# A conditioned attention and mixer block: the product of w_v and G as plain 32-bit matmuls, and every operation in a new place

## The chip, the core and the metric

The kernel runs on one core of a Trainium2 chip. The core has a matmul engine (PE in the profile, whose weight loads are shown apart as PEld), a vector engine (DVE), an engine for activation functions and scaled copies (ACT), a general engine (POOL), and an engine that here only issues DMA transfers (SP). Each takes its own instructions in the order in which the program gives them, and waits at an instruction until what it needs has been done elsewhere. Operands lie in on-chip memory, and matmul results in the accumulator banks (PSUM). The metric is the device time of one execution in microseconds (us).

## The reference

The input is x with 2048 rows (tokens) of 512 columns, a conditioning vector c, and the weights of two blocks. Cut to what matters:

```python
mod = (silu(c) @ w_mod).reshape(1, 6, 1, -1)           # sa, ca, ga, sb, cb, gb
h = layernorm(x) * (1 + ca) + sa
q, k, v = h @ wqkv, split into 32 heads of 16 columns
pq, pk = phi(q), phi(k)                                # phi(t) = t + 1 where t > 0, else exp(t); + 1e-6
kv = einsum("bhsd,bhse->bhde", pk, v);  z = pk summed over the tokens
o = (pq @ kv) / (pq . z + 1e-6)                        # head by head
x = x + ga * (o @ wo)
h = layernorm(x) * (1 + cb) + sb
z = gelu(h @ w_in);  z1 = z[:, :688];  z2 = layernorm(z[:, 688:])
g = w_sp @ z2 + b_sp                                   # w_sp is 2048 x 2048, over the tokens
out = x + gb * ((z1 * g) @ w_out)
```

## The kernel before, in words

The 2048 tokens are 16 row tiles of 128. A product that must keep the precision of 32-bit numbers is made of three: each operand is split into a high part, which is the number in the narrower 32-bit format that PE takes at its fast rate (`F32R`), and a low part, the rest; PE accumulates high times high, high times low and low times high (`mm3`, L113 to L115). A split costs a copy on ACT (L130) and a subtraction on DVE (L131), or variants of the two. A few products use plain 32-bit operands (`F32`) instead and have one matmul in the program: the modulation column `pcol` (L197), and the column means of the weights, `wm` (L335).

The stages, in the order of the program:

1. Start. w_mod gives the scale 1 + ca as a column; w_k and w_q are scaled, freed of their means and split (`mean_mm` L335, then DVE L339, then ACT L343). The first matmuls wait for the first transfers.
2. First block, per row tile: the k and q projections (`kp`, `qp`), phi, and, instead of v, G = the sum over all tokens of h (transposed) times pk, a 512 x 512 matrix that stays in accumulators (`g`).
3. After the last tile, kv = w_v (transposed) times G. Only the blocks of one head are wanted, so it is computed for four groups of 128 columns (`kv_mm`, L724 to L734: four 128-row parts `dc` of the inner dimension, four groups `g`) and masked (`kv_mask`). w_v is scaled by 1 + ca and split beforehand (`v_hi` L514, `v_lo` L518); G is split in `gh` (L702). Then kv is multiplied with w_o into m.
4. Attention output, per tile: o times m into `po`, the residual, the second layer norm, transposes, z = gelu(h2 times w_in) in two halves: z1 (L667) and z2 (`zz`, L673), layer norm of z2, and both parked in DRAM (`zd`, `z1d`). The z1 halves of the last four tiles come later (`z_late`, L872).
5. The spatial product w_sp times z2, partly plain (`Pq`) and mostly by a scheme of seven products for eight (`prod`, L956) whose operands are sums of quarters (L927 to L946); then u = z1 times the result, transposed through DRAM.
6. u times w_out (`pout`), the residual, and the output.

Nothing reorders the work. A table of two-letter names with numbers, `ORDER` for stages 1 to 4 and `ORDER3` for 5 and 6, is read from left to right; each name runs one small function, whose instructions go to the end of their engines' rows. On SP, where all transfers are issued, a transfer behind one that waits for a buffer waits with it. A second table, `SLOTS`, says which buffer of a pool each new tile takes, and so whose last use it has to wait for. The names that the prediction speaks of: `lw` loads a part of w_k or w_q and `ly` a transposed tile of x, `mr` is the column mean of a weight, `k`, `q` and `ki`, `km` belong to the projections and their weights, `kv` is the product above, `mS` and `mB` split and broadcast a modulation vector (`yh`, `yl`, then `pmod` on PE and `mod` on ACT), `g1` and `g2` are the two gelus, `d1`, `d2` and `at`, `ht` the denominator and transposes.

Of the kernel before, what the change touches and what calls it, by code (L numbers as in the profile page):

```python
# [14 lines left out]
P = 128  # L15
# [11 lines left out]
def block_kernel(ctx: ExitStack, tc: tile.TileContext, x, x_t, w_qkv, w_o, w_in, w_sp, b_sp, w_out,  # L27
# [3 lines left out]
    def pool(name, bufs, space=None, stack=None):  # L31
        if space is None:
# [21 lines left out]
        "md": "0321302313123113212312131223112131213121",  # L54
        "ta": "05431205413424204325214140532535530214014342402145025153545241503",
        "s4": (
            "076541237401267541720364615230745163074530516351065306174305264164034217563421602745032640137563"
            "017423156230764123756103625417502163256701423574635017624137135726417513064231570364712603742056"
            "34706145702614352634521670341065723410"
        ),  # L60
        "psb": "10101010101010101010110101010101010",
        "zs": "0fe123d4cba9876523d483ca9473b2dca74b2dc724d9b7c9dbc9dbc9dbc90fe165d83a4270b9c6158ef",
        "tb": (
            "065412360541631520641326542362361232134614206320606346536132613136256106313012161350420435610253"
            "256442405454132144140101063004414252053461"
        ),
        "pst": "01011010101110101",
        "st": (
            "032102312302102310232020312031320120310123102310230231131010231023102031301202130123031231012031"
            "0210"  # L70
        ),
        "ws": "0101",
        "pso": "010101001001110101011010110100101010010101010101",
        "tq": "ncedba987654mjihlkgf01327nm8gjbfcd69k0n83ebhfi4lajgmc9",
# [25 lines left out]
    def f(ap):  # L100
        return ap.bitcast(F32)
# [412 lines left out]
    def v_hi(kc):  # L514
        if not WV:
            WV.append(sb("ws", [P, 2, KC, D], F32R, "wv"))
        nc.scalar.activation(WV[0][:, 0, kc], RAW["qkv", 2, kc // 2][:, kc % 2, :], AF.Copy, scale=COL[1][:, kc:kc + 1])

    def v_lo(kc):
        nc.vector.scalar_tensor_tensor(WV[0][:, 1, kc], RAW["qkv", 2, kc // 2][:, kc % 2, :], COL[1][:, kc:kc + 1],  # L520
                                       f(WV[0][:, 0, kc]), op0=OP.mult, op1=OP.subtract)
# [19 lines left out]
    def win_lo(h, kc, eng=nc.gpsimd):  # L541
# [21 lines left out]
        "vh": v_hi, "vl": v_lo, "lW": load_win,  # L563
# [160 lines left out]
    def kv_mm(dc):  # L724
        if dc == 0:
            KV["kv"] = ps("o", [P, KC, P], "pkv")
        p, last = KV["kv"], dc == KC - 1
        for g in range(KC):
            sl = slice(g * P, (g + 1) * P)
            mm(p[:, g], WV[0][:, 0, dc, sl], GH[dc][:, 0, sl], start=dc == 0 and g == 0, stop=False,  # L730
               skip_group_check=True)
            mm(p[:, g], WV[0][:, 0, dc, sl], GH[dc][:, 1, sl], start=False, stop=False, skip_group_check=True)
            mm(p[:, g], WV[0][:, 1, dc, sl], GH[dc][:, 0, sl], start=False, stop=last and g == KC - 1,
               skip_group_check=True)  # L734
# [48 lines left out]
    def hx_lo(t):  # L783
# [16 lines left out]
        lm1,0 lm1,1 si du1 du2 du3 du4 cm1,0 lm1,2 cm1,1 cm1,2 lm1,3 cm1,3 mc lw1,0 du5 mr1,0 mr1,1 ly1 th1  # L800
        tl1 ce1 lw1,1 mr1,2 mr1,3 ly0 th0 tl0 ly2 th2 wf1,3 qh1,3 qg1,3 lw0,0 tl2 lw0,1 wf1,1 mr0,0 mr0,1
        qh1,1 qg1,1 mr0,2 wf1,0 qh1,0 lx0 mr0,3 lm0,1 s10 yp0,1 ki1,3 ki1,1 lm0,0 yp0,0 ki0,3 ki0,1 ki0,0
        kj0,1 wf1,2 lm0,2 yp0,2 ki1,0 kj1,1 lm0,3 bh0 kj0,3 qh1,2 kj1,3 ki1,2 ly5 qd1,0 wf0,0 wf0,1 wf0,3
        ya0,1 kj1,0 yp0,3 ya0,2 ya0,3 ki0,2 qh0,1 qd1,2 th5 kj1,2 qh0,0 qg0,0 kj0,0 lx1 kj0,2 lx2 s12 bh2 cr0
        ce0 qd0,1 qh0,3 s11 lx5 wf0,2 qh0,2 qg0,2 by0 kr1 bp1 by1 km2 kr2 qd0,3 qm0 tl5 km5 by2 kr0 bh1 lw2,0
        by3 bp0 ba1 ly3 s15 bx1 qr0 bb1 bp2 ba2 bl0 be1 k15 th3 bp3 qm1 qr1 ba3 bx0 lM2 tl3 km3 qm3 lx4 ka2
        ka0 s14 lx3 s13 bl1 k20 vh1 ly9 k40 ka1 lo0 th9 tl9 kr3 ly4 kh0 kl0 th4 mV2,0 mV2,1 k22 li bb0 be0 qm2
        k21 q12 bh3 gm0 tl4 ly8 k41 ks0 kh1 km4 qm4 bl2 q13 qm5 k42 ks1 ka3 k14 q22 q42 kl1 gm1 ly6 th6 kh2
        kl2 lo1 k25 k23 th8 k45 k43 mS2 q15 tl8 q14 bl3 k24 mB2 tl6 lx6 q24 lx9 ks2 ks3 kh3 qa0 k44 ks4 s16
        s19 ks5 lx8 kh4 km8 vh0 wg3 s18 km6 k16 bh9 bh5 bl5 bh4 gm2 lw2,1 q44 ly7 th7 tl7 kl3 kl4 q25 kh5 bh6  # L810
        bl4 qm6 q16 q45 k26 k46 ks6 bl9 ly12 lx7 ly11 th11 kh6 s17 ly10 q26 k18 th12 kl6 gm3 gm4 bh7 qa1 kl5
# [8 lines left out]
        kl14 bl14 lW0,2 ks15 wh0,2 mS4 zx mS3 gm13 zs bh15 zr d12 cv kh15 lX3 bl15 d10 wl0,1 kl15 d22 vb d20  # L820
        gm14 d13 gm15 gh0 gh1 gh2 q113 mB3 kv0 at2 wl0,2 gh3 d11 kv1 kv2 lW1,0 d23 mB4 wh1,1 wl1,1 kv3 kx q213
        qm15 q115 lW0,3 wh0,3 at0 d21 lW1,2 ae0 mm0 me0 ae2 mm2 me2 qm14 q114 wl0,3 at1 ae1 mm1 me1 d14 mm3
        at3 ae3 me3 d15 wh1,2 wl1,2 d24 lX0 wo0 x10 wh1,0 wl1,0 ap4 wo3 x13 wo1 h20 w02 wh1,3 wl1,3 q215 lX1
        d25 ht0 he0 w12 lX4 d17 x12 am4 ap5 ah4 al4 h22 hp2 q214 x11 am5 ah5 lX8 q413 h23 hm2 za0 zb0 g20 z00
        g10 wo4 al5 d16 h21 d19 hp3 wo5 d110 hh2 hl2 d27 d26 ht1 he1 z12 g22 q414 zl0 x14 ap6 h24 hm3 x15 z01
        g11 ap7 z02 hh3 hl3 hp4 d210 zn0 zp0 h25 g12 z13 g23 am6 ah6 hm4 hh4 am7 q415 d115 d18 z11 hp5 al6 ah7
        hl4 l5 lX7 z14 al7 d29 lX6 lX9 g21 ap10 zl2 d28 g24 zl4 d112 z04 hm5 hh5 hl5 ap8 d215 zn2 wo7 x17 g14
        h27 hp7 am8 ah8 al8 lX12 am10 z05 g15 zl3 z15 zh2 zp2 zo2 zl1 zh0 d212 d111 ah10 ap9 hm7 hh7 hl7 g25
        z03 al10 zl5 zn3 lX10 d211 wo6 x16 zp3 ap12 ap11 g13 am9 ah9 al9 zn4 d113 h26 hp6 z17 wo8 x18 z07 wo9
# [266 lines left out]
    def out_store(t, c0=0, c1=D):  # L1096
# [100 lines left out]
```

## Time and profile before

| | us |
|---|---|
| median of 3 runs | 620.19 (620.17 to 620.83) |
| span of the profiled execution, first to last instruction | 617.3 |
| PE busy in the span | 611.1 |
| DVE busy | 473.3 |
| ACT busy | 364.3 |
| POOL busy | 217.1 |

Of the profiled execution only the span is given, and its own device time isn't. The median lies 2.9 us above the span; that stands for what lies around it. The granted clock of PE was 1.000 in the mean. DMA moved 105.7 MB. A row of a view names the line of the kernel, the engine, the operation and the tile; a matmul's bar is longer than the distance to the next one, because matmuls overlap, so the pace of a row of matmuls is read from starts, or from the length of a stretch divided by their number.

### The profile page before, as it was taken

The page shows a single profiled execution, that of the slowest core. Times are in us where ns is not written, and L with a number is a line of the kernel's source. Part 1 is how long each engine was busy: PE and PEld are TensorE (multiplying, and loading weights), DVE is VectorE, ACT ScalarE, POOL GpSimd, SP SyncE. Part 2 cuts the span into 40 slices and gives each one's busy share as a digit, 9 for nine tenths or more (in the row PEclk, how much of TensorE's full clock was granted, in tenths as well). Part 3 has the DMA queues.
Part 4 walks back from the last instruction along what each step waited for, and adds up shares of the span by engine and source line. Part 5 has one row for each costly group of instructions (what it writes and reads, how often), then busy time and mean ns, then how long its engine had stood idle before and what let it go on. Part 6 is the DMA issues. An engine that isn't in the chain of part 4 may idle for free.

```text
span 617.3 us, 9528 instructions
## 1 busy us (share of the span) xinstructions
PE 611.1 (99%) x3375; PEld 558.2 (90%) x3375; DVE 473.3 (77%) x881; ACT 364.3 (59%) x619; POOL 217.1 (35%) x180
## 2 busy tenths in 40 slices
PE   8999999999999999999999999999999999999997
PEld 6788888888899999999999999999999999998886
DVE  2989889897788878988767998867757777866462
ACT  3876768565656667666566466475656564654530
POOL 0843444637676476755240012123122121300000
PEclk9999999999999999999999999999999999999999
DMA  8453323261244778646658736366455667899941
GB/s 286 174 192 117 106 69 104 75 198 40 64 121 116 206 186 223 178 136 172 194 172 277 287 133 180 104 191 181 139 171 141 196 187 167 293 280 262 291 177 68
DMA packets 91022, 105.74 MB, mean 171 GB/s; under 512 B 57088, under 2 KB 57600, under 8 KB 90976
## 3 DMA queue, kind: packets, MB, share of 16 engines
q1 hardware_dynamic: 90976, 105.15, 56.9%
q8 instruction: 26, 0.43, 0.3%
q14 instruction: 20, 0.16, 0.1%
HBM read 66.07 MB, written 25.95 MB: 149 GB/s over the span
## 4 chain that ended last, share of the span: by engine, by line
PE 89%; DVE 4%; DMA 3%; ACT 1%; SPq 1%; issue 1%; POOL 0%; DVEq 0%; ACTq 0%
PE P L956 29%; PE z L662 12%; PE Pq L956 5%; PE pout L114 3%; PE pout L113 3%; PE pout L115 3%; PE z L872 2%; PE g L113 2%; PE g L115 2%; PE qp L114 2%; PE qp L115 2%; PE qp L113 2%; PE g L114 2%; PE kp L113 2%; PE kp L114 2%; PE po L115 2%
## 5 line engine op out<-in xcount | busy, mean ns | idle before, releaser
L956 PE MATMUL P<-z,f 128*128 128x344 f32 x672 | 110.9, 320 | 0.2 <-DVE us L980 0.2
L662 PE MATMUL z<-win,ht 128*128 128x344 f32 x672 | 107.6, 320 | 0.2 <-DVE ht L301 0.2
L662 PEld LDWEIGHTS z<-win,ht 128*128 128x128 f32 x672 | 106.2, 188 | 1.1 <-DVE ht L301 0.5
L956 PEld LDWEIGHTS P<-z,f 128*128 128x128 f32 x672 | 106.6, 188 | 0.6 <-DVE us L980 0.5
L946 POOL TENSOR_TENSOR f<-raw_wsp,f 128x512 fp32r<-128x512 f32 x28 | 42.1, 1513 | 168.5 <-ACT f L943 159.3
L257 POOL TENSOR_TENSOR mv<-ve,mhalf 128x1 f32<-128x1 f32 x48 | 36.2, 757 | 43.1 <-DVE ve L256 40.7
L946 DVE TENSOR_TENSOR f<-sa,f 128x512 fp32r<-128x512 f32 x42 | 32.7, 788 | 18.8 <-ACT f L943 18.8
L943 ACT ACTIVATE f<-sa 128x512 fp32r<-128x512 f32 x42 | 26.1, 628 | 27.5 <-DVE sa L933 9.7
L943 ACT ACTIVATE f<-raw_wsp 128x512 fp32r<-128x512 f32 x56 | 34.1, 624 | 12.6 <-PE P L956 4.7
L281 ACT COPY uca<-ucb 128x768 uint16<-128x768 uint16 x32 | 31.9, 1063 | 13.5 <-DMA ucb<-uca 13.4
L480 POOL TENSOR_TENSOR pksum<-pksum,tk 128x512 f32<-128x512 f32 x15 | 23.1, 1539 | 41.4 <-DVE tk L452 34.2
L114 PE MATMUL pout<-wout,ut 128*128 128x512 f32 (+1 forms) x85 | 32.4, 381 | 0.0
L113 PE MATMUL pout<-wout,ut 128*128 128x512 f32 (+1 forms) x85 | 32.4, 381 | 0.0
L115 PE MATMUL pout<-wout,ut 128*128 128x512 f32 (+1 forms) x85 | 32.3, 380 | 0.0
L956 PE MATMUL Pq<-z,wsp 128*128 128x344 f32 x192 | 30.8, 321 | 0.0
L956 PEld LDWEIGHTS Pq<-z,wsp 128*128 128x128 f32 x192 | 30.6, 188 | 0.0
L271 ACT COPY uca<-us 128x768 uint16<-128x768 uint16 x32 | 25.0, 828 | 7.5 <-PE P L956 5.6
L591 POOL TENSOR_TENSOR prod<-pq,zrep 128x512 f32<-128x512 f32 x16 | 21.3, 1348 | 13.0 <-DMA z1d<-z 4.6
L113 PE MATMUL po<-m,pt 128*128 128x512 f32 x64 | 25.3, 396 | 0.0
L113 PE MATMUL g<-pkhl,hhl 128*128 128x512 f32 x64 | 25.3, 395 | 0.0
L115 PE MATMUL po<-m,pt 128*128 128x512 f32 x64 | 25.3, 395 | 0.0
L115 PE MATMUL g<-pkhl,hhl 128*128 128x512 f32 x64 | 25.2, 394 | 0.0
(260 smaller groups left out, 1556.7 us busy)
## 6 DMA issues: line engine op xcount, KB each, us to landing
raw_wsp<-in_w_sp SPq DMA_DIRECT2D x32, 512.0 KB, 4.3
ud<-uca SPq DMA_DIRECT2D x16, 384.0 KB, 2.7
ur<-ud SPq DMA_DIRECT2D x16, 384.0 KB, 4.6
z1d<-z SPq DMA_DIRECT2D x16, 344.0 KB, 2.6
zd<-zz SPq DMA_DIRECT2D x16, 344.0 KB, 2.7
z1r<-z1d SPq DMA_DIRECT2D x16, 344.0 KB, 3.9
xt<-in_x_t SPq DMA_DIRECT2D x16, 256.0 KB, 2.9
x<-in_x SPq DMA_DIRECT2D x16, 256.0 KB, 2.7
```

What stands on the lines that cost most here:

```text
L113: mm(o, a_hi, b_hi, start=first, stop=False, **kw)
L114: mm(o, a_hi, b_lo, start=False, stop=False, **kw)
L115: mm(o, a_lo, b_hi, start=False, stop=last, **kw)
L257: nc.gpsimd.tensor_tensor(mv[:, 1:2], ve, mhalf, op=OP.pow)
L271: nc.scalar.copy(pl[:, h], v[:, :, h])
L281: copy(o[:, :, h], plt[:, h * n:(h + 1) * n].rearrange("p a b -> p (a b)"))
L480: nc.gpsimd.tensor_add(pksum, pksum, PK[t])
L591: nc.gpsimd.tensor_mul(pr, PQ[t], KV["z"])
L662: mm(p[:, b, :HB], a[:, i, kc], win[h][:, j, kc, b * HB:(b + 1) * HB], start=kc == 0 and k == 0, stop=kc == KC - 1 and k == 2)
L943: nc.scalar.activation(SF[p, h, k][:, 0], s_src(p, h, k), AF.Copy)
L946: eng.tensor_sub(SF[p, h, k][:, 1], s_src(p, h, k), f(SF[p, h, k][:, 0]))
L956: mm(B[key][:, :HB], a[:, x_], b[:, y_], start=i == 1, stop=i == n)
```

## The change

w_v and G are no longer split. `v_hi` becomes `v_scale`, one scaled copy on ACT into a plain 32-bit tile; `v_lo` on DVE is gone. `gh` is one copy on ACT out of the accumulator; its subtraction on DVE is gone. `kv_mm` has one matmul of plain 32-bit operands per group and part, 16 in all, where it had 48. Everything after it (mask, split of kv, product with w_o) is as it was. The tables `ORDER`, `ORDER3` and `SLOTS` are new from end to end. The line numbers fall by 3 above the changed functions and by 7 to 11 behind them.

```diff
     SLOTS = {
-        "md": "0321302313123113212312131223112131213121",
...
+        "md": "0230201332132113212312131213223211121321",
...
-    def v_hi(kc):
+    def v_scale(kc):
         if not WV:
-            WV.append(sb("ws", [P, 2, KC, D], F32R, "wv"))
-        nc.scalar.activation(WV[0][:, 0, kc], RAW["qkv", 2, kc // 2][:, kc % 2, :], AF.Copy, scale=COL[1][:, kc:kc + 1])
-
-    def v_lo(kc):
-        nc.vector.scalar_tensor_tensor(WV[0][:, 1, kc], RAW["qkv", 2, kc // 2][:, kc % 2, :], COL[1][:, kc:kc + 1],
-                                       f(WV[0][:, 0, kc]), op0=OP.mult, op1=OP.subtract)
+            WV.append(sb("ws", [P, KC, D], F32, "wv"))
+        nc.scalar.activation(WV[0][:, kc], RAW["qkv", 2, kc // 2][:, kc % 2, :], AF.Copy, scale=COL[1][:, kc:kc + 1])
...
     def gh(dc):
-        GH[dc] = sb("zs", [P, 2, D], F32R, f"gh{dc}")
-        hi_lo(GH[dc][:, 0], GH[dc][:, 1], G[dc // 2][:, dc % 2, :])
+        GH[dc] = sb("zs", [P, D], F32, f"gh{dc}")
+        nc.scalar.activation(GH[dc], G[dc // 2][:, dc % 2, :], AF.Copy)
...
-        p, last = KV["kv"], dc == KC - 1
         for g in range(KC):
             sl = slice(g * P, (g + 1) * P)
-            mm(p[:, g], WV[0][:, 0, dc, sl], GH[dc][:, 0, sl], start=dc == 0 and g == 0, stop=False,
-               skip_group_check=True)
-            mm(p[:, g], WV[0][:, 0, dc, sl], GH[dc][:, 1, sl], start=False, stop=False, skip_group_check=True)
-            mm(p[:, g], WV[0][:, 1, dc, sl], GH[dc][:, 0, sl], start=False, stop=last and g == KC - 1,
-               skip_group_check=True)
+            mm(KV["kv"][:, g], WV[0][:, dc, sl], GH[dc][:, sl], start=dc == 0 and g == 0,
+               stop=dc == KC - 1 and g == KC - 1, skip_group_check=True)
...
     ORDER = """
-        lm1,0 lm1,1 si du1 du2 du3 du4 cm1,0 lm1,2 cm1,1 cm1,2 lm1,3 cm1,3 mc lw1,0 du5 mr1,0 mr1,1 ly1 th1
-        tl1 ce1 lw1,1 mr1,2 mr1,3 ly0 th0 tl0 ly2 th2 wf1,3 qh1,3 qg1,3 lw0,0 tl2 lw0,1 wf1,1 mr0,0 mr0,1
...
+        si lm1,0 lm1,1 du1 lm1,2 du5 lm1,3 lw1,0 ly1 du4 du2 cm1,0 cm1,1 lw1,1 ly0 lw0,0 cm1,2 du3 cm1,3 mc
+        ly2 th1 lw0,1 th0 lx0 mr1,1 mr1,0 ce1 lm0,1 tl1 lm0,0 mr1,3 lm0,2 mr1,2 lx5 th2 mr0,0 ly3 tl0 wf1,3
...
```

What the tables move is seen in the engines' rows. On PE, at the product of w_v and G (`pkv`; `pmod` is the broadcast of a modulation vector, `tpp` a transpose, `qp` a projection, `g` the last tile of G). Before:

```order
L240 MATMUL pmod_1610<-yh_1517,ones 128x512
L241 MATMUL pmod_1610<-yl_1518,ones 128x512
L730 MATMUL pkv<-gh_1599,wv 128x128
L732 MATMUL pkv<-gh_1599,wv 128x128
L733 MATMUL pkv<-gh_1599,wv 128x128
...
L308 MATMUL tpp_1628<-ident,pq_658 128x128 x4
L730 MATMUL pkv<-gh_1602,wv 128x128
...
L240 MATMUL pmod_1670<-yh_1510,ones 128x512
L241 MATMUL pmod_1670<-yl_1511,ones 128x512
L730 MATMUL pkv<-gh_1634,wv 128x128
```

After the change:

```order
L237 MATMUL pmod_1582<-yh_1499,ones 128x512
L238 MATMUL pmod_1582<-yl_1500,ones 128x512
L110 MATMUL g_596<-pkhl_1522,hhl_1518 128x512
...
L722 MATMUL pkv<-gh_1603,wv 128x128 x4
L722 MATMUL pkv<-gh_1605,wv 128x128 x4
L305 MATMUL tpp_1623<-ident,pq_659 128x128 x4
L722 MATMUL pkv<-gh_1628,wv 128x128 x4
L722 MATMUL pkv<-gh_1632,wv 128x128 x4
L110 MATMUL qp_1649<-wq_161,ht_1219 128x512
```

Three matmuls per group and part became one, and both broadcasts now stand ahead of the last tile of G instead of in front of and within the product.

On ACT, where the first gelu of the second stage comes (L673, after the change L666; `eq` is the exponential of phi, L449, now L446; ACT_TABLE_LOAD loads the table of a function that isn't at hand). Before:

```order
L271 COPY xph_1933<-h_2_1930 128x512 x2
L448 ACTIVATE eq_1937<-tq_1762,tiny 128x512
L449 ACTIVATE eq_1937<-eq_1937 128x512
L297 ACTIVATE pt_1952<-xpp_1923 128x512
L673 ACT_TABLE_LOAD
L673 ACTIVATE zz_1987<-z_0_1962 128x688
L667 ACTIVATE z_0_2014<-z_0_1989 128x688
L271 COPY xph_2039<-h_3_1957 128x512 x2
L297 ACTIVATE ht_2_2058<-xph_1933 128x512
```

After the change:

```order
L666 ACT_TABLE_LOAD
L666 ACTIVATE zz_1927<-z_0_1866 128x688
L294 ACTIVATE pt_1957<-xpp_1889 128x512
L660 ACTIVATE z_0_1972<-z_0_1932 128x688
L445 ACTIVATE eq_1981<-tq_1771,tiny 128x512
L446 ACT_TABLE_LOAD
L446 ACTIVATE eq_1981<-eq_1981 128x512
L294 ACTIVATE ht_2_1984<-xph_1912 128x512
...
L445 ACTIVATE eq_2059<-tq_1730,tiny 128x512
L446 ACTIVATE eq_2059<-eq_2059 128x512
L666 ACT_TABLE_LOAD
L666 ACTIVATE zz_2062<-z_2_2034 128x688
```

The last two exponentials stood ahead of the first gelu and now stand behind it, so ACT has four table loads in the program where it had two: the first at the start, then these three.

On SP, at the start (`raw_qkv` with 0 or 1 is a half of w_k or w_q, 512 KB; `xt` a transposed tile of x, 256 KB). Before:

```order
L145 DMA raw_qkv_0_204<-in_w_qkv 128x1024
L151 DMA xt_211<-in_x_t 128x512
L145 DMA raw_qkv_1_218<-in_w_qkv 128x1024
L151 DMA xt_222<-in_x_t 128x512
L151 DMA xt_227<-in_x_t 128x512
L145 DMA raw_qkv_0_235<-in_w_qkv 128x1024
L145 DMA raw_qkv_1_238<-in_w_qkv 128x1024
```

After the change:

```order
L142 DMA raw_qkv_0_181<-in_w_qkv 128x1024
L148 DMA xt_183<-in_x_t 128x512
L142 DMA raw_qkv_1_198<-in_w_qkv 128x1024
L148 DMA xt_200<-in_x_t 128x512
L142 DMA raw_qkv_0_202<-in_w_qkv 128x1024
L148 DMA xt_216<-in_x_t 128x512
L142 DMA raw_qkv_1_220<-in_w_qkv 128x1024
```

The third half (the first of w_q) now goes out ahead of the third tile of x.

More of the change, by code (lines that the diff above doesn't have):

```diff
@@ L53, in block_kernel @@
     SLOTS = {
-        "md": "0321302313123113212312131223112131213121",
-        "ta": "05431205413424204325214140532535530214014342402145025153545241503",
+        "psb": "01010010110101011001010101110101010",
+        "ws": "0101",
+        "zs": "652ae0d47193efc48078bdc3f0c41c837f4804b70c4f8c74b874b87478b563a9c142f76bd80e524c5b8",
+        "md": "0230201332132113212312131213223211121321",
+        "st": "1032310123201203121012023123101203312010320102130121030121132031201301321032302123012103123130213232",
+        "ta": "35431250425335452403510402315431342551010102053124513343154154253",
+        "pst": "01000100010101110",
+        "tb": (
+            "654310256143263402613142401402553254063650200462040534126361436415263411265125554031512365640413"
+            "634453124432040533003110161634330211245601"
+        ),
         "s4": (
-            "076541237401267541720364615230745163074530516351065306174305264164034217563421602745032640137563"
-            "017423156230764123756103625417502163256701423574635017624137135726417513064231570364712603742056"
-            "34706145702614352634521670341065723410"
-        ),
[L61 to L74, printed above, removed]
+            "376542173154332034567166537020716471620073367047214230257146503571640731532754613046235614032113"
+            "740274567150323741260345320453607124071465046743560123064372612704153526701534276541203045167242"
+            "32165471064765042701140761213650474026"
+        ),
+        "pso": "101010110101101001010101010010101010101011010101",
+        "tq": "7b94j532fincel806k17adm4gej6h9bic2f53kjgbka57286eh1d2l",
         "z1": "0000000000000000",
@@ L820, in block_kernel @@
[L820 to L829, printed above, removed]
@@ new lines, in block_kernel @@
+        kx wh1,2 wh0,3 wl0,2 mm2 mm0 d21 mm1 mm3 at3 wl0,3 qm14 wl1,2 ae2 me0 q115 wl1,1 at1 lW1,0 me3 ae0 me1
+        me2 ae3 q213 wo0 q114 ae1 d15 wo3 wo1 d24 x10 w02 x13 ap4 h20 wh1,0 wh1,3 ht0 wl1,0 d25 he0 wl1,3 w12
+        za0 x12 ap5 zb0 am4 ah4 h22 hp2 al4 x11 g20 am5 q413 z00 ah5 wo4 g10 h23 hm2 q214 hh2 h21 q414 hl2 hp3
+        al5 d16 lX5 wo5 d18 d27 d26 ht1 he1 z12 q215 g22 ap7 z01 x14 hm3 ap6 hh3 d110 g11 x15 hl3 h24 z02 z13
+        am7 hp4 d210 g12 lX7 h25 hm4 d19 am6 hp5 hh4 hl4 g23 ah7 z11 q415 zl2 al7 lX6 d115 ah6 hm5 z14 z04 hh5
@@ new lines, in block_kernel @@
+        d28 g21 d29 al6 hl5 zl1 d112 zl3 g24 ap8 wo7 ap9 g14 zn2 d215 z05 am8 ah8 al8 ap10 zl0 x17 h27 z15 g15
+        zp2 lX12 d111 zh2 hp7 am10 zn0 d113 d212 d211 zn1 g25 hm7 wo8 ah10 hh7 lX8 zh0 ap12 zo2 zl5 wo6 zl4
+        hl7 zn3 x16 am9 al10 z03 x18 g13 ap11 zn5 lX9 z07 h26 ah9 z17 hp6 h28 al9 lX10 hp8 am11 zp0 l5 ah11
+        al11 wo9 am12 d213 g17 x19 hm8 wo10 zh1 g27 hh8 hm6 ap13 hl8 zl7 zo0 hh6 ah12 wo11 h29 zh5 zp1 z08 hp9
+        g18 x110 z18 hl6 lX13 zn4 lX11 h210 d114 hm9 z16 al12 hh9 zn7 hl9 g28 ap15 hp10 am13 zl8 z19 d214 g26
@@ L838, in block_kernel @@
+        zp10 aH0,0 aL1,0 mB5 zp6 aL0,0 zp11 g215
     """
@@ L1161, in block_kernel @@
+        wm15,0,256 ot14 wm15,256,512 ot15,0,256 ot15,256,512
     """
```

154 lines of the change are left out of this document (76 added, 78 removed).

## The prediction

> **What bounds the kernel now.** I read the page's first rows and the shares of the chain of waits first:
>
> ```profile
> span 617.3 us, 9528 instructions
> PE 611.1 (99%) x3375; PEld 558.2 (90%) x3375; DVE 473.3 (77%) x881; ACT 364.3 (59%) x619; POOL 217.1 (35%) x180
> PE 89%; DVE 4%; DMA 3%; ACT 1%; SPq 1%; issue 1%; POOL 0%; DVEq 0%; ACTq 0%
> ```
>
> PE is busy for 99% of the span. So the time is the sum of PE's matmuls, plus the few places where PE stands still; an edit is worth something only if it shortens PE's row or one of these places, and costs something only if it makes a new one. The view of what PE waited for names them:
>
> ```profile
> PE warm L175 <- POOL tiny L127: 1.0, 1, 1.0
> PE z L872 <- ACT mod L243: 0.5, 1, 0.5
> PE wm L335 <- DMA raw_qkv<-in_w_qkv: 0.5, 1, 0.5
> PE P L956 <- DVE us L980: 0.2, 1, 0.2
> PE z L662 <- DVE ht L301: 0.2, 1, 0.2
> ```
>
> Columns are the total in us, times, and the longest. By stretches (duration, then PE's busy time first):
>
> ```profile
> 0.00:20.00 20.00, 18.25 (x77) 13.36 (x78) 7.88 (x17) 8.64 (x15) 4.93 (x11) 1.00 0.86 308
> 180.00:210.00 30.00, 29.83 (x180) 28.34 (x179) 27.50 (x54) 19.10 (x32) 14.27 (x13) 1.00 0.52 137
> 300.00:320.00 20.00, 19.32 (x121) 18.60 (x120) 12.58 (x26) 12.01 (x20) 7.82 (x6) 1.00 0.58 173
> ```
>
> PE stands still for 1.75 us at the start, 0.17 between 180 and 210, 0.68 between 300 and 320, and 0.2 in the P stage. The rest of the missing time is the tail, which the change leaves. In 180 to 210 DVE is busy for 27.50 of 30 us (third pair of numbers): nothing there has much room.
>
> **The product of w_v and G.** Its 48 matmuls become 16. The rows of the old and of the nearest plain 32-bit product, by durations (least, median, most):
>
> ```profile
> L733 PE MATMUL pkv<-gh,wv x16: 272/275/278, 150.3 to 156.2; 128*128 128x128 f32 x16
> L733 PEld LDWEIGHTS pkv<-gh,wv x16: 191/192/192, 150.2 to 156.1; 128*128 128x128 f32 x16
> L197 PE MATMUL pcol<-sil,raw_mod x32: 272/273/553, 4.7 to 9.3; 128*128 128x128 f32 x32
> L197 PEld LDWEIGHTS pcol<-sil,raw_mod x32: 190/191/333, 4.7 to 9.1; 128*128 128x128 f32 x32
> 156.16 0.28 PE L733 MATMUL pkv<-gh,wv 128*128 128x128 f32 x1
> 156.27 0.45 PE L113 MATMUL qp<-wq,ht 128*128 128x512 f32 x1
> 8.36 1.17 PE L197 MATMUL pcol<-sil,raw_mod 128*128 128x128 f32 x9
> ```
>
> `pcol` is a plain 128 x 128 product, 16 of them in the code, and the trace has 32 instructions: a plain matmul is two instructions. The last pkv matmul starts 0.11 us ahead of the next instruction; over the whole product the starts are 0.1115 apart, so 48 x 0.1115 = 5.35 us. For `pcol`, nine in 1.17 us, of which the last one's bar is 0.273: (1.17 - 0.27) / 8 = 0.112. So 16 x 2 x 0.112 = 3.58, and the gain is **1.77 us**. No row here runs faster than 0.11 per matmul, so this is near the most. The bound on the other side comes from a wider plain product:
>
> ```profile
> 14.44 3.67 PE L335 MATMUL wm<-raw_qkv,cbr 128*128 128x512 f32 x8 [0.53 <-DMA raw_qkv<-in_w_qkv]
> 18.11 5.60 PE kp L420 x24
> ```
>
> At 512 columns a plain instruction takes 3.67 / 8 = 0.459 us and a fast one 5.60 / 24 = 0.233. If that ratio of 2 held at 128 columns too, 32 x 0.223 = 7.1 us, a loss of 1.8. I take the gain, since `pcol` has the very shape, and 0.459 / 4 = 0.115 says that the plain one's time goes with its columns.
>
> Off PE the change removes four subtractions for w_v and four for G:
>
> ```profile
> L520 DVE SCALAR_TENSOR_TENSOR wv<-raw_qkv,col,wv x4: 742/826/909, 81.7 to 126.3; 128x512 fp32r<-128x512 f32 x4
> L131 DVE TENSOR_TENSOR gh<-g,gh x4: 680/691/692, 149.1 to 152.4; 128x512 fp32r<-128x512 f32 x4
> ```
>
> That is 4 x 0.826 + 4 x 0.691 = 6.1 us of DVE, in stretches where PE never waited. I cost it at nothing. The copies on ACT stay. The mask and split of kv lie behind the product as before, and in both orders the projection `qp` of a tile stands behind it on PE and covers them.
>
> **The start.** SP issues the first half of w_q, for which PE waits 0.53 us above, behind a transfer of x that now goes out after it:
>
> ```profile
> 4.51 2.37 SPq L151 DMA_DIRECT2D xt<-in_x_t  x2
> 6.93 1.18 SPq L145 DMA_DIRECT2D raw_qkv<-in_w_qkv  x2
> 2.00:14.00 12.00, 11.67 (x57) 9.02 (x56) 1.94 (x6) 2.76 (x7) 0.00 (x0) 1.00 0.92 319
> L420 PE MATMUL kp<-wk,ht x24: 393/395/798, 17.5 to 23.3; 128*128 128x512 f32 x24
> ```
>
> The queues are full there (0.92 of all engines' time, 319 GB/s), so 256 KB fewer ahead of it are 262 / 319 = 0.82 us, and an issue slot of 2.37 / 2 = 1.2 us is saved. The wait of 0.53 goes. Behind it one `kp` matmul lasts 798 ns instead of 395: 0.40 us in which its weight wasn't split yet. In the new order the first projections stand between the means of w_q and so have other work ahead of them; part of this goes too. I take 0.65, between 0 (the half of w_q arrives, and the split of w_k becomes the wait) and 0.93.
>
> **The table loads.** The first gelu now comes ahead of the last two exponentials, and ACT loads a table twice more:
>
> ```profile
> 184.11 0.72 ACT L448 ACTIVATE eq<-tq,tiny 128x512 f32<-128x512 f32 x1
> 185.52 0.63 ACT L297 ACTIVATE pt<-xpp 128x512 fp32r<-128x512 f32 x1
> 186.17 1.28 ACT L673 ACT_TABLE_LOAD   x1
> 187.47 0.74 ACT L673 ACTIVATE zz<-z 128x688 f32<-128x688 f32 x1
> 186.00:206.00 20.00, 19.83 (x117) 18.48 (x116) 17.71 (x36) 12.20 (x22) 11.37 (x10) 1.00 0.52 139
> 194.85 0.76 DVE pq L452
> 203.54 0.74 PE L662 MATMUL z<-win,ht 128*128 128x344 f32 x3 [0.17 <-DVE ht L301]
> ```
>
> One load is 1.28 us. A pair of activations for one exponential takes from 184.11 to 185.52, 1.41 us. So 2 x 1.28 + 2 x 1.41 = 5.4 us come into a stretch of 20 us in which ACT (the fourth pair) has 20 - 12.2 = 7.8 free: it fits in the sum. What counts is who waits for each piece. `pq` (phi, on DVE) needs the exponential and was in the chain that ended in PE's wait at 203.54; behind it on DVE stand the split of the transposes and the next layer norm. Laying the new row of ACT over these durations from the start of the first z product, the second tile's transposes are ready 14.15 us behind it where PE comes at 14.1, the first tile's at 17.7 against 17.9, the third's at 23.7 against 24.8, the fourth's at 32.1 against 32.4. In return the gelu no longer waits for the exponentials, and the old wait (0.17 shown, some 0.3 by the starts) goes. I take **0**, between -0.3 and, with both loads on the path, +2.6.
>
> The load's row says that a switch costs its bar alone: the activation before ends at 185.52 + 0.63 = 186.15 and the one behind starts at 187.47. The Trainium skill ("ScalarE: Activation LUTs", section "What ACT_TABLE_LOAD costs") counts a drain of about 1.38 us on top of the load, 2.66 for every switch; there is no such gap here. If it came, the sum would be up to 2 x 1.38 = 2.8 us higher.
>
> **The wait at 317.** Here PE waits for a broadcast whose high part took the buffer of a z2 tile still being parked:
>
> ```profile
> 311.41 5.31 DMA zd<-zz
> 317.67 0.40 PE L240 MATMUL pmod<-yh,ones 128*128 128x512 f32 x1
> 318.21 0.50 PE L241 MATMUL pmod<-yl,ones 128*128 128x512 f32 x1
> 318.55 0.31 PE L872 MATMUL z<-win,ht 128*128 128x344 f32 x1
> 319.40 0.74 PE L872 MATMUL z<-win,ht 128*128 128x344 f32 x3 [0.53 <-ACT mod L243]
> ```
>
> The two `pmod` matmuls start 0.54 apart, where the second and its successor are 0.34 apart: 0.2 lost for the low part, some 0.3 ahead of the first, and 0.53 behind, for ACT's copy. Now the high part's buffer was last held by tile 6's z2 and the low part's by tile 10's; by the rows I reckon the parts ready 1 to 1.5 us sooner against PE. The copy behind `pmod` stays, since the late z product takes its accumulator. I take -0.3, between 0 and -0.5.
>
> **The P stage.** One wait of 0.2 there came from a chain through a transfer:
>
> ```profile
> 479.55 4.88 DMA raw_wsp<-in_w_sp
> 485.53 0.59 DVE us L980
> ```
>
> In the new order the operands of a product stand further ahead of it (the sums and splits of w_sp, a median of some 3.8 us of PE's work instead of 1.9), so this wait should go; but the first products of the stage use a w_sp half that is loaded late, into a buffer that a gelu frees, with some 3.5 us to spare. I take 0, between -0.2 and +3.
>
> **The sum**, against the profiled execution: 617.3 - 1.77 - 0.65 + 0 - 0.3 + 0 = 614.6 us of span. The median of the runs stands 2.9 above that span, so the forecast is **617.5 us**.
>
> **Rivals.**
>
> *Both table loads land on the path.* For it: DVE is nearly full there, and the margins that I worked out are tenths. Against: ACT has 7.8 us free. Price 2.6: 620.1, no change.
>
> *ACT becomes the bound between 186 and 206, and the time is longer than before.* The two loads and the two exponentials stand between gelus that empty accumulators which PE wants again, so a late gelu stops PE itself. ACT would be busy for 12.2 + 5.4 = 17.6 of 20 us, as full as DVE, and its free time lay in pieces, each behind a wait for DVE. If none of the pieces can be used, 5.4 us come to the path: 614.6 + 5.4 + 2.9 = 622.9. It decides from 4.0 us on the path, where the time passes 621.4.
>
> *A w_sp half comes late at the start of the P stage.* With the 3.5 us to spare used up, each further us is PE's; at +3 the time is 620.5, no change. Against it: a half takes 4 to 5 us to land (the row at 479.55), and the queue isn't full there.
>
> *The plain matmul at 128 columns is twice as slow,* as at 512: 3.6 us dearer than forecast, 621.1, no change. Against it stand the `pcol` rows. The Trainium skill ("TensorE: Matmul & The Clock Gate", section "Weight-path perf modes — Fast Weight Load (FWL) and DoubleRow") speaks against plain operands too: the fast weight load is for 128 weights of a type other than FP32. The weight loads above, 191 ns and 192, show no difference.
>
> *Only the product gains,* and the new places give as much as they take: 617.3 - 1.77 + 2.9 = 618.4, still faster.
>
> **How the numbers follow.** A measurement here tells 0.2%, 1.24 us, from no change: faster is below 618.95, slower above 621.43. The forecast with its own range (615.8 to 618.4) has 0.52, only the product 0.14, both loads on the path 0.12, ACT the bound 0.12, the late w_sp half 0.06, the slow matmul 0.04. Faster: 0.52 + 0.14 = 0.66. Slower: 0.12, and 0.02 of the late half. Same: the rest, 0.20. The low end takes every gain in full (-1.77 - 0.93 - 0.3 - 0.5 - 0.2 = -3.7, so 616.5 in the terms that I could price) and 0.7 for terms that I couldn't; the high end, 621.0, takes in both cases of no change and leaves out the slow side: 615.8 to 621.0.
>
> **What would show it.** In the changed kernel's profile: 32 pkv instructions 0.112 apart (right) or over 0.2 (wrong); no wait of PE for the w_q half, and no `kp` matmul of 800 ns; ACT's two loads with PE busy for 29.8 of the 30 us behind the first z product, or a wait there behind `ht`, `z` or `zz`; the two `pmod` 0.34 apart; no wait of P for w_sp's splits. A new wait of PE above 1 us anywhere makes the prediction wrong, and names the step.

## The result, and the profile after

The changed kernel takes 630.7 us (629.62 to 631.31) against 620.5 (620.17 to 622.09): 1.0157 times as long, with an interval of 1.0141 to 1.0174. The forecast was 617.5. The page of the changed kernel:

```profile
span 629.2 us, 9439 instructions
PE 613.4 (97%) x3359; PEld 555.4 (88%) x3359; DVE 476.6 (76%) x873; ACT 365.7 (58%) x621; POOL 216.0 (34%) x180
PE 41%; DMA 11%; DVE 8%; ACT 3%; issue 3%; POOL 2%; SPq 0%; DVEq 0%; ACTq 0%; POOLq 0%
```

What its PE waited for (total in us, times, longest), without the wait for `tiny`, which is 1.0 us as before, and without five more rows of 0.2 to 0.6 us:

```profile
PE z L655 <- ACT zz L666: 2.1, 3, 1.0
PE P L945 <- DVE us L969: 1.6, 1, 1.6
PE pout L112 <- DVE ut L1040: 1.6, 1, 1.6
PE pout L110 <- ACT ut L1034: 0.8, 1, 0.8
PE P L945 <- POOL f L935: 0.8, 1, 0.8
PE z L655 <- ACT ht L294: 0.8, 1, 0.8
PE wm L332 <- ACT cbr L326: 0.7, 1, 0.7
PE z L861 <- ACT mod L240: 0.7, 1, 0.7
```

PE's share of the chain that ended last fell from 89% to 41%. Beyond the wait for `tiny`, five rows of waits became thirteen, and no single one explains the loss. (The prediction's list shows four of the five; it leaves out 0.2 us for `cbr`.) The product itself did what was foretold:

```profile
L722 PE MATMUL pkv<-gh,wv x32: 272/275/275, 151.0 to 154.9; 128*128 128x128 f32 x32
```

There are 32 instructions, and their starts are 0.112 us apart in the median, as forecast. To put waits that the bars hide on one scale, I take for each form of matmul the median distance from its start to the next start, and call the rest of each distance a wait (a stretch without waits can come out a little below zero). The medians alone add up to 607.8 us before and 606.0 after: PE's own work fell by the 1.8 us of the forecast. The rest, by stretches of each kernel's own time:

| us | before | after |
|---|---|---|
| 0 to 40 | 2.2 | 1.8 |
| 40 to 160 | -0.1 | 1.2 |
| 160 to 220 | 0.5 | 1.5 |
| 220 to 300 | 0.1 | 2.7 |
| 300 to 340 | 1.2 | 1.9 |
| 340 to 380 | 0.0 | 0.1 |
| 380 to 560 | 0.9 | 6.4 |
| 560 to the end | 0.1 | 3.2 |
| all | 4.8 | 18.8 |

So 14.0 us of waits came and 1.8 us of work went: 12.2 against a span that grew by 11.9. (By the medians the kernel is 10.2 us longer; the first profile of the kernel before was of a quick execution, as a run below shows.) Stretches of both kernels, before first and then after (duration, then PE, PEld, DVE, ACT, POOL busy):

```profile
210.00:300.00 90.00, 90.00 (x517) 84.77 (x516) 73.87 (x165) 56.35 (x95) 58.16 (x50) 1.00 0.68 187
330.00:380.00 50.00, 50.00 (x318) 50.00 (x317) 47.15 (x91) 25.02 (x54) 5.86 (x4) 1.00 0.62 210
480.00:570.00 90.00, 89.82 (x530) 85.72 (x530) 67.52 (x116) 52.06 (x88) 14.47 (x10) 1.00 0.82 233
570.00:617.30 47.30, 43.92 (x206) 36.09 (x204) 19.88 (x42) 13.72 (x25) 0.00 (x0) 1.00 0.55 182
```

```profile
210.00:300.00 90.00, 87.24 (x491) 80.44 (x490) 74.30 (x158) 52.19 (x89) 54.73 (x50) 1.00 0.67 175
330.00:380.00 50.00, 50.00 (x318) 49.95 (x317) 43.01 (x84) 26.30 (x55) 4.09 (x5) 1.00 0.69 243
480.00:570.00 90.00, 87.28 (x529) 84.11 (x529) 58.87 (x101) 54.84 (x87) 16.50 (x13) 1.00 0.71 193
570.00:629.20 59.20, 53.69 (x246) 43.30 (x244) 27.58 (x58) 18.74 (x36) 0.00 (x0) 1.00 0.72 226
```

The transfers move the same bytes, and only ACT has more instructions than before: the two table loads, 2.6 us. But DVE, though it is rid of 6.1 us of subtractions, is busy for 476.6 us where it was 473.3, so its other instructions take longer than they did; the last section says where. PE is idle more, at many places, for work that comes a little too late.

Two of these waits, seen closely. On ACT at 213 (start, duration, bracket: idle before and its end), then on DVE at 572:

```profile
209.50 0.64 ACT L294 ACTIVATE pt<-xpp 128x512 fp32r<-128x512 f32 x1 [0.77 <-PE z L655]
212.69 0.63 ACT L294 ACTIVATE ht<-xph 128x512 fp32r<-128x512 f32 x1 [2.55 <-DVE xph L278]
213.23 0.30 ACT L593 ACTIVATE den<-den,tiny 128x32 f32<-128x32 f32 x1
213.44 0.72 ACT L666 ACTIVATE zz<-z 128x688 f32<-128x688 f32 x1
```

```profile
572.57 0.69 DVE L1087 TENSOR_TENSOR x<-x,pout 128x512 f32<-128x512 f32 x1 [4.84 <-DMA x<-x1d]
573.18 0.55 DVE L1040 TENSOR_TENSOR ut<-ur,ut 128x384 fp32r<-128x384 f32 x1
```

The gelu at 213.44 empties an accumulator for which PE waits from 213.2 to 214.2. It stands in ACT's row behind the copy `ht`, for which ACT stood idle for 2.55 us until DVE was done. The split `ut` at 573.18, for which PE waits 1.6 us, stands behind the first output addition, for whose x DVE stood idle for 4.84 us. This is one shape of the loss: work that PE needs stands in its engine's row behind an instruction that waits for something PE doesn't need yet.

### The profile page after: what moved, and what is told of

Read it like the earlier page. It is cut to its first block, busy times and chain, and to the rows that moved or that the text cites. A ratio compares the mean times of both kernels' runs of the same rounds, so it can differ in the third digit from the quotient of the medians.

```text
span 629.2 us, 9439 instructions
## 1 busy us (share of the span) xinstructions
PE 613.4 (97%) x3359; PEld 555.4 (88%) x3359; DVE 476.6 (76%) x873; ACT 365.7 (58%) x621; POOL 216.0 (34%) x180
## 4 chain that ended last, share of the span: by engine, by line
PE 41%; DMA 11%; DVE 8%; ACT 3%; issue 3%; POOL 2%; SPq 0%; DVEq 0%; ACTq 0%; POOLq 0%
PE P L945 21%; PE Pq L945 5%; PE z L655 4%; DMA ud<-uca 3%; DMA ucb<-uca 3%; PE z L861 2%; PE pout L112 2%; PE pout L110 2%; PE pout L111 2%; DMA xph<-xph 2%; DVE xph L278 2%; DMA x1d<-xr 1%; DMA raw_wsp<-in_w_sp 1%; DMA x<-x1d 1%; DVE bst L249 1%
## 5 line engine op out<-in xcount | busy, mean ns | idle before, releaser
L935 POOL TENSOR_TENSOR f<-raw_wsp,f 128x512 fp32r<-128x512 f32 x28 | 39.3, 1407 | 176.3 <-ACT f L932 131.0
L254 POOL TENSOR_TENSOR mv<-ve,mhalf 128x1 f32<-128x1 f32 x48 | 38.7, 807 | 57.1 <-DVE ve L253 46.4
L935 DVE TENSOR_TENSOR f<-sa,f 128x512 fp32r<-128x512 f32 x42 | 30.1, 725 | 10.8 <-ACT f L932 10.8
L1034 ACT ACTIVATE ut<-ur 128x384 fp32r<-128x384 f32 x32 | 15.0, 517 | 25.7 <-PE pout L1083 9.7
L935 DVE TENSOR_TENSOR f<-raw_wsp,f 128x512 fp32r<-128x512 f32 x28 | 22.0, 789 | 6.0 <-ACT f L932 6.0
L112 PE MATMUL po<-m,pt 128*128 128x512 f32 x64 | 25.4, 397 | 0.1
L110 PE MATMUL qp<-wq,ht 128*128 128x512 f32 x64 | 25.3, 396 | 0.0
```

Of the source, the lines that this page charges most:

```text
L110: mm(o, a_hi, b_hi, start=first, stop=False, **kw)
L112: mm(o, a_lo, b_hi, start=False, stop=last, **kw)
L254: nc.gpsimd.tensor_tensor(mv[:, 1:2], ve, mhalf, op=OP.pow)
L935: eng.tensor_sub(SF[p, h, k][:, 1], s_src(p, h, k), f(SF[p, h, k][:, 0]))
```

## The experiments

**The product alone, and the places alone.** The kernel before with its own order and the new product:

```diff
-    (v_hi, v_lo, gh, kv_mm as before; ORDER with vl0 to vl3)
+    (v_scale, gh, kv_mm as changed; ORDER without vl0 to vl3, nothing else moved)
```

> The kernel before with its own order and buffers, and only the product changed: w_v and G unsplit, 16 plain matmuls, the four subtractions for w_v taken out of the order. Theory A (the product gives what it was priced at, and the new places take the rest): 620.5 - 1.8 = 618.7 us. Rival B (the shorter product moves all that follows against the transfers and makes the waits itself): 622 us or more, with new waits of PE behind 156 us.

Measured: 620.84 us, 0.9997 times the kernel before (0.9985 to 1.0008). Neither: it isn't slower, but the 1.8 us aren't there either; at most 0.9 of them can be. What its PE waited for (without `tiny` and two rows of 0.2 us):

```profile
PE wm L335 <- DMA raw_qkv<-in_w_qkv: 1.1, 2, 0.7
PE P L948 <- DVE us L972: 0.8, 1, 0.8
PE z L864 <- ACT mod L243: 0.5, 1, 0.5
PE P L948 <- POOL f L938: 0.4, 1, 0.4
PE pm L115 <- DVE kvh L131: 0.3, 1, 0.3
PE pout L115 <- DVE ut L1043: 0.3, 1, 0.3
PE z L658 <- ACT zz L669: 0.3, 1, 0.3
```

(The first profile of the kernel before has three of these: the half of w_q with 0.5 us, the copy of `mod` with 0.5 and `us` with 0.2.) By the starts its waits are 8.3 us against 4.8. PE comes to the mask of kv, to a gelu, to a w_sp part and to the output splits earlier than they are ready. To see whether the first profile of the kernel before was typical, it was run once more:

> The kernel before once more, for a second profile. The median of its runs has a span of 619.1 us, 1.8 us more than the profiled execution that the prediction used. If that execution was a quick one, this one has a span of 618.5 to 620 us and 1 to 2 us more of small waits of PE, at places where the changed kernels have waits too (start, 485, 536, 564 us).

Its span was 617.7 us and its time 619.4, with 5.0 us of waits by the starts, at the same places as in the first profile (start, 203, 317, 485). So the expectation was wrong: a second execution also shows few waits, and none at 536 or 564. But both profiled executions lie below the median, so a median one of this kernel hasn't been seen in detail, and of the 3.5 us of waits that the product alone seems to add, part is that its profile is not of a quick execution. In all later runs the time is 1.7 to 2.0 us above the span, so the span of 617.3 stands for some 619.1, and the 2.9 us that the prediction put around the span were 1.8 and 1.1 of luck (1.8 against the median of the later runs).

The new order with the old product was run twice, since the four subtractions that split w_v have to stand somewhere in DVE's row:

```diff
-vh1 ...            vh0 ...            vh3 ...            vh2 ...
+vh1 vl1 ...        vh0 vl0 ...        vh3 vl3 ...        vh2 vl2 ...
```

> The changed kernel with its new order and buffers, but with w_v and G split again and 48 matmuls in the product; the low parts of w_v come right behind the high parts. Theory A: 630.7 + 1.8 = 632.5 us. Rival B: most of the loss gone, 621 to 625 us.

Measured: 646.72 us, 1.0431 times before (1.0394 to 1.0467), far beyond both. PE's first large wait in its profile is this one:

```profile
PE kp L110 <- DVE tk L428: 3.9, 1, 3.9
```

Then with the four spread over later places in the row:

> The new order with the split product again, as before, but the four subtractions for w_v are spread over places in DVE's row like those of the kernel before, instead of right behind the high parts. Theory A (product and places add up): 632.5 us. If the time stays near 646.7, the new order has no room for 3.3 us of DVE wherever they stand.

Measured: 636.60 us, 1.0285 times before (1.0230 to 1.0339), between the two that were expected. So in the new order the plain product is worth 6 to 8 us against the split one, and in the old order nothing that can be measured. Product and places don't add up. The likely reason, which no run shows by itself, is the 6.1 us less of DVE: they count where operands are finished shortly before their use, as in the new order (below), and don't where they are finished long before. And the place of four instructions of some 0.83 us moved the time by 9 to 10 us.

**Which half of the order.** Each table of places was put together with the other half of the old one. The buffers of the first half were renamed so that each tile that is still needed lies where the second half expects it, and in the first of the two kernels one low part (`zo11`) was moved to the front of the second table, because the new first half counts on it there.

```diff
 new_first:   ORDER of the change,  ORDER3 of before,  plain product
 new_second:  ORDER of before,      ORDER3 of the change,  plain product
```

> The changed kernel's first table of places (everything up to the second gelus) with the old second table (spatial product and output), the plain product, and buffers joined so that each live tile lies where the second table wants it. Theory A: by the starts of PE's matmuls the waits up to 330 us grew by 5.1 us and those behind it by 8.8; so 620.5 - 1.8 + 5.1 = 623.8 us. Rival C (the waits behind 330 us are a follow-on of the first half, such as tiles that are parked late): about 630 us.

> The old first table of places with the changed kernel's second table, the plain product, and buffers joined in the same way. Theory A: 620.5 - 1.8 + 8.8 = 627.5 us. Rival C: 618.7 to 621 us, since the first half is as it was.

Measured: 626.86 us (1.0096, 1.0081 to 1.0111) and 627.07 (1.0102, 1.0086 to 1.0117). Each half costs about 6 us by itself, together 12 where the whole change costs 10. Rival C falls: the second half is late on its own account, also behind the old first half. By the starts, the P stage's products from 380 us on wait for 2.5 us with the new first half, as in the kernel with the product alone, and for 5.8 with the new second, where the changed kernel has 5.9. Theory A is right for the second kernel and 3 us too low for the first, whose wait at 213 us is 2.25 us where the changed kernel has 0.97, with slow matmuls behind it (last section).

**Table loads.** The exponentials were put ahead of the first gelu again:

```diff
-x11 g20 am5 q413 z00 ah5 wo4 g10 h23 hm2 q214 hh2 h21 q414 ... z12 q215 g22 ... q415
+x11 q413 q214 q414 q215 q415 g20 am5 z00 ah5 wo4 g10 h23 hm2 hh2 h21 ... z12 g22 ...
```

> The changed kernel with its last two exponentials, and the parts of phi behind them, moved ahead of the first gelu again: two table loads instead of four. Theory T (the two more table loads are on the path): 630.7 - 2.6 = 628.1 us or less. Theory D: the loads lie in ACT's free time, 630.7 within 0.7.

Measured: 636.83 us, 1.0263 (1.0243 to 1.0283): 6 us longer than the change, with two table loads less. Neither theory foresaw that. PE's new wait, at 187 to 189.4 us, the chain that leads to it (start, duration), and ACT's row behind the exponentials:

```profile
PE po L110 <- ACT pt L294: 2.5, 1, 2.5
```

```profile
183.47 0.61 DVE pq L449
184.11 0.73 ACT eq L445
184.87 0.63 ACT eq L446
185.50 0.62 ACT eq L445
186.14 0.64 ACT eq L446
187.42 0.78 DVE xpp L278 x2
```

```profile
186.79 1.28 ACT L666 ACT_TABLE_LOAD   x1
188.09 0.74 ACT L666 ACTIVATE zz<-z 128x688 f32<-128x688 f32 x1
188.73 0.62 ACT L294 ACTIVATE pt<-xpp 128x512 fp32r<-128x512 f32 x1
```

The two exponentials take 2.7 us on ACT between 184 and 187, ahead of the load, the gelu and the copy `pt` that PE waits for; the parts of phi stand on DVE ahead of the copies `xpp` that `pt` reads. In the changed kernel `pt` starts at 184.95, here at 188.73. So behind the first gelu the exponentials are in the better place of the two, loads included. What the loads cost there by themselves was not measured, since the exponentials moved with them.

**Undoing the shape.** Six names of the changed kernel were moved:

```diff
 ORDER
-hh5 d28 g21           hh9 zn7 hl9 g28           hh15 g213
+g21 hh5 d28           g28 hh9 zn7 hl9           g213 hh15
 ORDER3
-ss7,1,3 fh7,0,2 pr6,1,5 pr6,1,3 cd6,2      ot0 lx1 ur10 ul5 um14 ul4      ug15 uh11
+cd6,2 ss7,1,3 fh7,0,2 pr6,1,5 pr6,1,3      lx1 ur10 ul5 um14 ul4 ot0      uh11 ug15
```

> The changed kernel with six names moved in its tables, nothing else: three gelus that free an accumulator stand ahead of the copy of a transpose that they stood behind on ACT (waits of PE at 213, 266 and 317 us), one sum out of an accumulator stands ahead of the sum that waited for a late half of w_sp on DVE (532), one output addition stands behind a split that PE waited for (572), and one split stands ahead of a copy that waited for a transfer on ACT (609). Theory D (each of these waits is work that PE needs, standing in its engine's row behind an instruction that waits for something else): the waits by the starts of PE's matmuls are 1.24 + 1.24 + 0.42 + 1.73 + 1.82 + 1.09 = 7.5 us, so 630.7 - 7.5 = 623.2 us. Rival E (what is freed is late again right behind, since the chains through transfers and DVE set the pace): 628 to 631 us.

Measured: 627.21 us, 1.0115 (1.0097 to 1.0133): 3.5 us less by the medians, some 2.6 by the ratios, of 7.5. The waits at 213, 266, 317, 572 and 609 are gone, and the one at 532 fell from 1.73 to 0.68. Others came or grew:

```profile
PE z L655 <- DVE ht L298: 1.5, 1, 1.5
PE P L944 <- DVE us L977: 0.9, 1, 0.9
PE P L944 <- POOL f L934: 1.3, 2, 0.8
```

The first is at 238, where the change had none. By the starts the waits fell from 18.8 to 15.1 us, but those of the P stage's products from 380 us on stayed (5.6 against 5.9). So the shape is a cause, and both theories were half right: what is freed arrives at the next chain early and waits there for about half of it.

The same with the product in the old order, at its own waits:

```diff
 ORDER
-ly2 th2 wf1,3 qh1,3 qg1,3 lw0,0      +lw0,0 ly2 th2 wf1,3 qh1,3 qg1,3
 ORDER3
-fh6,0,2 fl5,1,3 cs5,1                +cs5,1 fh6,0,2 fl5,1,3
-ug13 uq13 uh4 wm0 ot0 ul4 uh5        +uh4 uh5 ug13 uq13 wm0 ot0 ul4
```

> The kernel before with the plain product and four names moved: the first half of w_q goes out ahead of the third tile of x, one copy out of an accumulator stands ahead of a copy that waits for a late half of w_sp (PE's wait at 485 us), and two splits stand ahead of a copy that waits for a transposing transfer (wait at 564). Theory D: 620.8 - 0.9 - 1.0 - 0.5 = 618.4 us, faster than both kernels. Rival E: 620 to 621 us.

Measured: 620.73 us, 1.0002 (0.9992 to 1.0013): rival E. The wait at 564 is gone, and that for the half of w_q fell from 1.1 us to 0.7, but at 485 PE now waits for the next thing, the low part of w_sp from POOL:

```profile
PE P L947 <- POOL f L937: 1.2, 2, 0.8
```

**Does PE set the pace at all?** Matmuls were left out of the kernel with the old order and the plain product: in Pq the product of w_sp's low part with z2's high part (the expectation names the wrong factor), in G the product with h's low part.

```diff
-        for x_, y_ in ((0, 0), (0, 1), (1, 0)):                    # Pq only
+        for x_, y_ in ((0, 0), (0, 1)):
-            mm3(G..., a hi, a lo, b hi, b lo, ...)                 # G only
+            mm(o, a hi, b hi, ...); mm(o, a hi, b lo, ...)
```

> The kernel before with the plain product, and in the plain part of the spatial product (Pq, 326 to 365 us) the third of the three matmuls left out (low part of z2 apart, its operands are still made): 64 matmuls of 0.159 us, 10.2 us less on PE just ahead of the P stage. If PE's row alone sets the time: 620.8 - 10.2 = 610.6 us. Theory P (the chains that feed PE have a pace of their own, and PE had been running right behind them): 615 us or more, with PE waiting in the P stage for parts of w_sp.

> The kernel before with the plain product, and in G the third of the three matmuls left out for every tile (the low part of h is still made): 64 matmuls of 0.231 us, 14.8 us less on PE, spread over the first 150 us. If PE's row alone sets the time: 620.8 - 14.8 = 606.0 us. Theory P: 612 us or more, with new waits of PE for DVE and ACT.

Measured without Pq's third: 619.74 us, 0.9993 times before (0.9977 to 1.0008). Of 10.2 us that PE no longer had to do, nothing arrived at the end. Its waits:

```profile
PE P L948 <- ACT t_0r L903: 5.9, 1, 5.9
```

The two stretches, before and in the long wait:

```profile
330.00:354.00 24.00, 24.00 (x152) 23.61 (x152) 22.93 (x41) 10.17 (x23) 1.47 (x1) 1.00 0.83 297
354.00:366.00 12.00, 5.28 (x19) 4.19 (x18) 11.79 (x27) 7.32 (x17) 0.00 (x0) 0.74 0.26 102
```

PE ends Pq at 354.9 and stands until 360.8. DVE is busy for 22.93 of 24 us and then 11.79 of 12: it makes the differences and splits of z2's quarters that the first products of the P stage need, almost without a break. By the starts, PE's waits between 340 and 380 are 9.6 us; some 2 of these are matmuls behind the wait that run at the lower clock (0.74, third number from the end), so not all of the 10.2 us is DVE's. In the kernel before, DVE is as full there (47.15 of 50 us in 330 to 380, above) and PE shows no wait, because Pq happens to last as long as DVE does. Two rows were full, and I saw the one that is read first.

Without G's third: 612.28 us, 0.9884 (0.9867 to 0.9900), so 7.9 of 14.8 us by the medians came through. The rest went into waits such as these:

```profile
PE g L492 <- DVE pkhl L473: 1.6, 1, 1.6
PE qp L113 <- DVE tq L431: 1.4, 1, 1.4
```

**Is it the head start?** For each of the 98 tiles of w_sp sums that the P stage uses, I took the start of the first matmul that reads it less the end of the subtraction that finishes it. The kernel before has a median lead of 4.6 us (2.3 at the lowest quarter), 6 tiles under 1 us; the changed kernel 2.0 (1.0), and 23 under 1 us. The halves follow their tables: 3.8 us in the kernel with the new first half, 2.0 in that with the new second. If the short leads were a late start, 4 us of extra PE work ahead of the stage would lengthen them all:

```diff
     def prod(p, h, k):
+        if (p, h, k) == (1, 0, 1):
+            B[p, k] = bank(BANK[k], "P1_1")
+            for _ in range(25):
+                mm(B[p, k][:, :HB], SF[p, h, k][:, 0, 0], t_of(0, k)[:, 0], start=True, stop=True)
```

> The changed kernel with the first matmul of the P stage issued 25 times more into the accumulator that it then starts afresh: 4.0 us more of PE ahead of the P stage, in which the other engines can get ahead. Theory L (the operands of the P stage are only finished too late by up to 1.7 us, and a head start lasts): the waits between 380 and 551 us, 5.7 us by the starts, go: 630.7 + 4.0 - 5.7 = 629.0 us. Theory P (a head start is lost again, since buffers and transfers let nobody run ahead): 634.7 us.

Measured: 637.62 us, 1.0290 (1.0267 to 1.0313): theory P, and 3 us more. The median lead between 360 and 400 us rose from 2.0 to 4.2; between 400 and 440 it was 2.6 (1.9 in the change), and from 440 on 2.0 again. The head start is mostly gone after 40 us and wholly after 70, and by the starts the stage's products from 380 us on wait for 5.7 us where the change has 5.9. So the lead of 2 us belongs to the new rows and buffers. A likely reason is that a producer can't run further ahead, because the buffer that it writes or the accumulator that it empties comes free only so late; no run shows that, and whether the row order or the choice of buffers holds the lead there was not tried apart. The 3 us more are in other places, of which the largest is behind the stage, where the change had 1.6:

```profile
PE pout L112 <- DVE ut L1044: 2.5, 1, 2.5
```

## Why the prediction was wrong, point by point

- **What bounds the kernel: the step that failed first.** "The time is the sum of PE's matmuls, plus the few places where PE stands still" holds as bookkeeping of one execution, but not as a rule for what an edit is worth. 10.2 us off PE ahead of the P stage were worth nothing, 14.8 us in the first stage 8, and 1.8 us in the product at most 0.9. An idle time of 0 says that the other engines' rows are not later than PE; it doesn't say by how much they are earlier. In 330 to 380 DVE was at 47.15 of 50 us, in a stretch for which I asked no view.
- **The product: -1.77.** As PE's work right: 32 instructions, 1.8 us less in the sum of medians. (The 0.459 us that it took for a plain matmul of 512 columns holds the last bar in full; the starts of `wm` are 0.43 apart, and 0.43 / 4 = 0.107 supports the same choice.) As time at the end wrong: 0.9997 (0.9985 to 1.0008). Costing the 6.1 us of DVE at nothing was right in the old order and, as far as the runs with the split product tell, wrong in the new one.
- **The start: -0.65.** PE's wait for the half of w_q is gone, as said. But the means now begin behind a wait of 0.7 us for `cbr`, where there was one of 0.2, and one `kp` matmul still starts 0.40 late and another 0.25. Waits in the first 40 us: 1.8 against 2.2, so about -0.4, inside its bounds; but the second profile of the kernel before has 1.9, so no more than -0.1 of it is sure.
- **The table loads: 0.** In 180 to 210 PE was busy for 29.92 of 30 us where it had been for 29.83. Right there, and the rival in which both loads land on the path falls. ACT as the bound between 186 and 206 falls too: it is busy for 14.32 of 20 us, not 17.6. All three loads of this stretch start and end within 0.02 us of their neighbours on ACT, so the drain of the Trainium skill ("ScalarE: Activation LUTs", section "What ACT_TABLE_LOAD costs") showed no cost here either.
- **The wait at 317: -0.3.** The two `pmod` now start 0.23 apart, and the wait for ACT's copy stays (0.69 us where it was 0.53), both as said. But just ahead PE loses 0.4 us to the split of a transpose on DVE and 0.3 to a gelu that stands behind the copy of one, so the stretch from 300 to 340 gives 1.9 us of waits instead of 1.2.
- **The P stage: 0. Here the largest term failed:** 380 to 560 went from 0.9 to 6.4 us, 5.9 of them at the stage's own products. I had read from the order that operands stand further ahead of their products (3.8 us of PE's work against 1.9). That distance was counted in the text, across engines. In time the operands were finished 2.0 us ahead instead of 4.6. How far an instruction stands ahead in a table said nothing here about when it was finished. What holds the operands back stays open (their buffers and their place in their own engine's row were not tried apart).
- **No term at all** for 210 to 300 (2.6 us more) and for the output stage (3.1 more). I had priced the places where the old kernel waited, and taken all others, where PE never waited, as covered. A new order moves every one of them.
- **The rivals.** None had the mechanism. The one that ended on the slow side put 5.4 us in one place; what came was 14 us in some sixteen places of 0.3 to 1.8. The range was built from the margins that I had worked out, and those that I hadn't worked out were given nothing.
- **2.9 us around the span:** 1.7 to 2.0, in every later run; the rest was that the profiled execution lay below the median.

## What to carry to other kernels

A bound read from busy shares is a bound for that stretch only if the second-fullest engine there has room: before pricing a saving, look at the fullest other engine stage by stage, and at the leads with which operands are finished. A schedule in which PE hardly waits has its value in these leads, and an order that is new everywhere must be judged by all of them, in time and on each engine, not by the waits that the old one had. Where a row of instructions is kept in order, anything that frees what the bound engine needs goes ahead of what waits for a transfer.

## What the runs showed of the hardware

After a wait PE can run slower for a while. In the kernel with the new first half PE stood 2.25 us at 213; the granted clock (third number from the end) before and behind it:

```profile
205.00:213.00 8.00, 8.00 (x53) 8.00 (x52) 6.69 (x13) 3.79 (x7) 4.20 (x5) 1.00 0.88 168
215.90:219.80 3.90, 3.89 (x15) 3.89 (x16) 3.41 (x10) 3.12 (x6) 3.61 (x4) 0.59 0.10 21
```

The matmuls start 0.287 us apart instead of 0.157, eleven of them: 1.4 us on top of the wait. Behind the wait of 5.9 us in the kernel without Pq's third the clock was 0.74 over the stretch, and in the new order with the split product right behind the high parts the matmuls behind the wait of 3.9 us were 0.43 apart instead of 0.23. The length of one wait doesn't decide it alone: 1.9 us was enough in the new order with the split product spread (clock 0.59 from 541 to 545), a wait of 2.2 us at 225 in the other kernel with the split product was followed by a clock of 1.00, and without G's third the clock was 0.61 from 137 to 141, behind waits of 0.4 and 0.6 us. The Trainium skill ("TensorE: Matmul & The Clock Gate", section "HAM oscillation — how this bites in real kernels") puts the limit at idle gaps of some 3.4 us; here one of 2.25 us was enough once, and one of 1.9.

A pair of 16-bit copies on DVE takes 0.8 us (at 188.34 in the kernel before) and up to 2.95 (at 189.54 in the kernel with the exponentials ahead) when it starts while POOL works, as here in the kernel with six names moved, on DVE and on POOL:

```profile
233.85 2.80 DVE L278 COPY xph<-xph 128x512 uint16<-128x512 uint16 x2 [1.97 <-DMA xph<-xph]
```

```profile
232.44 2.08 POOL L596 TENSOR_TENSOR pq<-pq,den 128x512 f32<-128x512 f32 x2
234.47 1.86 POOL L691 TENSOR_TENSOR z<-zz,z 128x688 fp32r<-128x688 f32 x1
```

The pair isn't slower at its work, it stands still: it ends at 236.65, 0.32 us behind the end of POOL's second instruction at 236.33, and the seven long copies of the changed kernel end 0.32 to 0.33 us behind the end of POOL's too. The Trainium skill ("GPSIMD Engine Reference", section "1. Specifications") names the interface that the two engines share. For an order that is kept by hand it means that a lead of 2 us can be used up by what stands beside it on POOL.

This is also where DVE's longer time comes from. Every DVE instruction of both kernels that lasts over 0.06 us longer than the quickest tenth of its form starts while POOL is at work. Together they last 34.9 us longer than those in the kernel before, 44.1 in the changed one, 48.7 in the one with the new first half and 33.4 in that with the new second. So it belongs to the new first half; how much of that half's 6 us it costs, no run shows.
